# Loading chunk A ahead of chunk C, and bringing one row to all partitions by DMA instead of a matmul

## The chip, the cores and the metric

The kernel runs on one core of a Trainium2 chip. The metric is device time in microseconds (us).

Engines are written as the profile writes them: PE (TensorE, matmuls), PEld (its weight loads), DVE (VectorE), ACT (ScalarE), POOL (GpSimd), SP (SyncE, which issues the DMAs). "L717" is line 717 of the kernel whose profile is shown; after the change the same statement may have another number.

## The reference, cut to what matters

```python
# x: [8, 3008, 256] fp32
X = np.fft.fft(x, axis=1); X = np.fft.fft(X, axis=2)
y = X.real.reshape(8 * 3008, 256)
g = y @ w_gate                       # w_gate, w_val: [256, 1536]
out = (g / (1 + np.exp(-g)) * (y @ w_val)) @ w_out
```

The kernel never forms the spectrum in full. It folds x by symmetry (POOL), multiplies with cosine and sine tables (PE) to get two half spectra P and Q, and uses that rows k and M-k of the real part are P+Q and P-Q. So each column tile of P and Q gives two sets of outputs, "plus" and "minus". The second transform is folded into the weights (Wp, Wq, Wm).

## The kernel before

The main loop runs over 24 tiles t of up to 512 columns and 12 blocks f of the hidden size: 288 *units*. A unit computes gate g and value v for plus (`part_a`) and for minus (`part_b`, one unit later), and between them PE does four or eight output matmuls of the tile before (`owork.run(4)`). From tile 2 on, six of the twelve units (nine in the last tiles) are *split*: value is made of an even part e and an odd part o, so that DVE does three cheap combinations and POOL does the multiplies. Only these need `bc`, the row d=0 of Q copied to all partitions.

```python
psG: 3 PSUM banks (g)   psV: 3 PSUM banks (v, e, o)   psO: 2 banks
SPLIT = (0, 2, 3, 5, 7, 9)

def part_a(u):                                   # (cut)
    g = psG.tile(...);  mm(g, Wp, 0, Pt, True, False);  mm(g, Wq, 0, Qt, False, True)      # L717
    if split(u):
        e = psV.tile(...);  mm(e, Wp, 1, Pt, True, True)
        o = psV.tile(...);  mm(o, Wm, 1, Qt, True, True)     # "v<-Qt,Wm" in the profile
        sg = silu(g)                                                                       # ACT
        es = bc[t] * w0[:, f] + e                                                          # DVE L732
        vp = es - 0.5 * o;  vm = es + 0.5 * o (columns reversed)                           # DVE L734, L736
        hp = sg * vp                                                                       # POOL L737
        return
    v = psV.tile(...);  mm(v, Wp, 1, Pt, True, False);  mm(v, Wq, 1, Qt, False, True)
    hp = silu(g) * v                                                                       # ACT, DVE L745
# part_b(u), one unit later: adds Wm @ Qt to g (and, if not split, to v)                   # PE L754
#   split: hm = silu(g) * vm on POOL (L759);   else hm = silu(g) * v on DVE (L763)

for i, u in enumerate(units):                    # (cut)
    t, f = u
    if f == 0 and split((t, SPLIT[0])):
        ps = psG.tile([P, T], F32, name="g")
        nc.tensor.matmul(ps[:, :w], sel, pq_tiles(t)[1][:, :w], start=True, stop=True)     # L854, the row matmul
        bc[t] = bcp.tile([P, T], F32, name="bc")
        nc.scalar.copy(bc[t][:, :w], ps[:, :w])                                            # L857
    if i == 10:
        loads.extend((("A", 1), fn) for fn in load_a(1, nc.sync))
    run_loads(3)                                 # issue the next three queued loads
    part_a(u)
    if owork: owork.run(4)
    if prev is not None: part_b(prev) ...
    if owork ...: owork.run(4)
    for what, j in fold_at.get(i, ()): fold_step(what, j, i)      # POOL folds, a step at a time
```

Chunk A of a batch is 20 loads into `XA` (2 MB), chunk C is 20 smaller ones for each of two batches into `XC`. The fold of chunk A of batch 1 is spread over units 13 to 24; its first step issues all loads that are still queued in front of it. `XA` is first used for weights; its last reader is a group of small matmuls in unit 9.

Of the kernel before, what the change touches and what calls it, by code (L numbers as in the profile page):

```python
# [12 lines left out]
F32 = mybir.dt.float32  # L13
I32 = mybir.dt.int32
BF16 = mybir.dt.bfloat16
# [16 lines left out]
def kernel(  # L32
# [8 lines left out]
    nc = tc.nc  # L41
    B, M, D = x.shape
    Dff = moe_w_gate.shape[1]
    P = 128
# [5 lines left out]
    T = 512  # L50
# [6 lines left out]
    nT = len(wide)  # L57
# [9 lines left out]
    def width(t):  # L67
        return wide[t]

    def tile_of(c):  # L70
        return max(t for t in range(nT) if t0[t] <= c)
# [6 lines left out]
    psG = ctx.enter_context(tc.tile_pool(name="psG", bufs=3, space=bass.MemoryType.PSUM))  # L78
# [12 lines left out]
    sel = const.tile([P, P], BF16, name="sel")  # L91
# [21 lines left out]
    def rows_at(b, row, ap):  # L113
        return bass.AP(tensor=x.tensor, offset=(b * M + row) * D, ap=ap)

    def up_block(b, j, n):
        return rows_at(b, 2 * j - 1, [[2 * D, n], [R * D, 4], [1, 2 * D]])

    def down_set(b, a, j, L, n):

        return rows_at(b, R * (a + 1) - 2 * j, [[2 * L * D, n], [-2 * D, L], [1, 2 * D]])
# [3 lines left out]
    def load_a(b, q):  # L125
        X3 = XA.rearrange("p a q d -> p a (q d)")
        return ([lambda h=h: q.dma_start(out=X3[LA * h:LA * (h + 1), 0:4, :],
                                         in_=up_block(b, JA - LA * h, LA)) for h in range(NA)] +
                [lambda a=a: q.dma_start(out=X3[:, 4 + a, :], in_=down_set(b, a, JA, LA, NA)) for a in range(4)])
# [16 lines left out]
    def fold_steps(eng, X, CE, BB, q, r, given=None):  # L146
        tt = eng.tensor_tensor
        S, Dd = given or (SDf[r, 0], SDf[r, 1])
        E, O = EOf[r, 0], EOf[r, 1]

        def sd(a, op):
            tt(SDf[r, a], X[r, 0:4, q, :], X[r, 7:3:-1, 1 - q, :], op=op)  # L152

        def even():
            tt(E[:, :, 0:P], S[:, :, P:0:-1], S[:, :, P:D], op=Alu.add)
            eng.tensor_copy(E[:, :, P:P + 1], S[:, :, 0:1])

        def odd():
            tt(O[:, :, 0:P], Dd[:, :, P:0:-1], Dd[:, :, P:D], op=Alu.subtract)

        def ab():
            tt(Af[r], EOf[r, :, 0:2, :], EOf[r, :, 2:4, :], op=Alu.add)  # L162

        def ce():
            tt(CE[r, q, :, 0, :], Af[r, :, 0, :], Af[r, :, 1, :], op=Alu.add)
            tt(CE[r, q, :, 1, :], Af[r, :, 0, :], Af[r, :, 1, :], op=Alu.subtract)

        def bb():
            tt(BB[r, q, 0], E[:, 0:4:3, 0:P], E[:, 2:0:-1, 0:P], op=Alu.subtract)
            tt(BB[r, q, 1], O[:, 0:2, 0:P], O[:, 2:4, 0:P], op=Alu.subtract)  # L170
            tt(BB[r, q, 1, :, 0:1], S[:, 3::-3, 0:1], S[:, 1:3, 0:1], op=Alu.subtract)

        return [lambda: sd(0, Alu.add), lambda: sd(1, Alu.subtract), even, odd, ab, ce, bb]
# [3 lines left out]
    def coef_a(b):  # L177
        if b not in coefA:
            coefA[b] = (cp.tile([P, 2, 2, 2, P + 1], BF16, name="CEa"),
                        cp.tile([P, 2, 2, 2, P], BF16, name="BBa"))  # L180
        return coefA[b]

    def coef_c(b):
        p = b if b < 2 else 1 + b // 2
        if p not in coefC:
            coefC[p] = (cp.tile([P, 2, 2, 2, P + 1], BF16, name="CEc"),
                        cp.tile([P, 2, 2, 2, P], BF16, name="BBc"))
        return coefC[p]
# [40 lines left out]
    for hi in range(2):  # L229
        q.dma_start(out=XC3[64 * hi:64 * hi + NCR, 0:2, :],  # L230
                    in_=rows_at(0, 2 * (P + 1) - 1 + 2 * hi * R, [[2 * D, NCR], [R * D, 2], [1, 2 * D]]))
    for hi in range(2):
        for a in range(2):
            q.dma_start(out=XC3[64 * hi:64 * hi + NCR, 2 + a, :],
                        in_=down_set(0, 3 - 2 * hi - a, JC, LC, NC_))
    q.dma_start(out=XC0[NCR:64 + NCR + 1:64, 0:2, 1],
                in_=rows_at(0, 0, [[2 * R * D, 2], [R * D, 2], [1, D]]))
# [21 lines left out]
    for i in range(6):  # L259
        ps = psO.tile([P, T], F32, name="o")  # L260
# [99 lines left out]
    opposite(0)  # L360
    nc.vector.memset(EOf[:, 1, :, P:P + 1], 0.0)
    nc.vector.memset(Tab[:, :, :, :, NOO - 1:NOO], 0.0)
    nc.vector.memset(sel[0:1, :], 1.0)
    vts(m2, pcol, scalar1=0.0, scalar2=-2.0, op0=Alu.not_equal, op1=Alu.mult)
    vts(sgn, half, scalar1=1.0 / 32, scalar2=1.0, op0=Alu.mult, op1=Alu.add)
    vts(wC, pc, scalar1=float(LC - 1), scalar2=-0.5, op0=Alu.is_equal, op1=Alu.mult)
# [146 lines left out]
    def pq_tiles(t):  # L513
        if t not in ptile:
            w = width(t) + B if t == nT - 1 else T
            ptile[t] = (pqp if t < nT - 1 else const).tile([P, w], BF16, name="Pt")
            qtile[t] = (pqp if t < nT - 1 else const).tile([P, w], BF16, name="Qt")
        return ptile[t], qtile[t]
# [78 lines left out]
    def whole_part(b, part):  # L597
        transform(b, part, (0,))
        transform(b, part, (1,))
# [20 lines left out]
    bcp = ctx.enter_context(tc.tile_pool(name="bc", bufs=2))  # L620
# [77 lines left out]
    SPLIT = (0, 2, 3, 5, 7, 9)  # L698
    SPLIT_END = (0, 1, 2, 4, 5, 7, 8, 10, 11)
    t_end = tile_of((B - 1) * H) + 1  # L700

    bc = {}

    def split(u):

        return 2 <= u[0] < nT - 1 and u[1] in (SPLIT if u[0] < t_end else SPLIT_END)
# [41 lines left out]
    def part_b(u):  # L748
        t, f = u
        w = width(t)  # L750
        Pt, Qt = pq_tiles(t)
        g, v = state.pop(u)
        for gv, ps in ((0, g), (1, v))[:1 if split(u) else 2]:
            nc.tensor.matmul(ps[:, :w], Wm[:, gv, f * P:(f + 1) * P], Qt[:, :w], start=False, stop=True,  # L754
                             skip_group_check=True)
        if split(u):
            sg = sgv.tile([P, T], F32, name="sgv")
            nc.scalar.activation(sg[:, w - 1::-1], g[:, :w], AF.Silu)  # L758
            nc.gpsimd.tensor_tensor(hts[t][1][:, f, :w], sg[:, :w], v[:, :w], op=Alu.mult)  # L759
            return  # L760
        sg = sgp.tile([P, T], F32, name="sg")
        nc.scalar.activation(sg[:, :w], g[:, :w], AF.Silu)  # L762
        nc.vector.tensor_tensor(hts[t][1][:, f, w - 1::-1], sg[:, :w], v[:, :w], op=Alu.mult)  # L763
# [21 lines left out]
    act_at = {}  # L785

    def run_loads(n):
        for _, fn in loads[:n]:
            fn()
        del loads[:n]  # L790

    def fold_step(what, i, unit):
        kind, b = what
        q, j = divmod(i, 7)
        if i == 0:
            run_loads(max((k + 1 for k, (w_, _) in enumerate(loads) if w_ == what), default=0))
        if j == 0:
            if kind == "A":
                queue[what] = fold_steps(nc.gpsimd, XA, *coef_a(b), q, slice(0, P))
            else:  # L800
                queue[what] = fold_steps(nc.gpsimd, XC, *coef_c(b), q, slice(64 if b == 1 else 0, P))
        queue[what].pop(0)()
        if q == 1 and j == 1:
            act_at.setdefault(unit + 2, []).append(what)

    def load_next(what):
        kind, b = what
        if kind == "A":
            if b + 1 < B:
                loads.extend((("A", b + 1), fn) for fn in load_a(b + 1, nc.sync))  # L810
        else:
            b = b // 2 * 2 + 2
            if b < B:
                loads.extend((("C", b), fn) for fn in load_c(b, nc.sync) + load_c(b + 1, nc.sync))
# [30 lines left out]
    loads = []  # L845
# [2 lines left out]
    owork = None  # L848
    for i, u in enumerate(units):
        t, f = u  # L850
        if f == 0 and split((t, SPLIT[0])):
            ps = psG.tile([P, T], F32, name="g")
            w = width(t)
            nc.tensor.matmul(ps[:, :w], sel, pq_tiles(t)[1][:, :w], start=True, stop=True)  # L854
            bc.pop(t - 2, None)
            bc[t] = bcp.tile([P, T], F32, name="bc")
            nc.scalar.copy(bc[t][:, :w], ps[:, :w])  # L857
        for fn in before.pop(i, ()):
            fn()
        if i == 10:  # L860
            loads.extend((("A", 1), fn) for fn in load_a(1, nc.sync))
        run_loads(3)
        part_a(u)
        if owork:
            owork.run(4)
        if prev is not None:
            part_b(prev)
            if prev[1] == nF - 1:
                owork = OWork(prev[0], hts[prev[0]])
                owork.run(4)  # L870
        if owork and not (prev is not None and prev[1] == nF - 1):
            owork.run(4)
        for what, j in fold_at.get(i, ()):
            fold_step(what, j, i)
        for what in act_at.pop(i, ()):
            load_next(what)
        if i in job_at:
            whole_part(*job_at[i])
        prev = u
# [35 lines left out]
```

## Time and profile before

Median 712.93 us (3 runs, 712.68 to 713.99).

The page of the profile: span, busy time of PE and POOL, and the busy tenths of 40 slices of 17.8 us each:

```profile
span 712.3 us, 13268 instructions
PE 679.5 (95%) x4369; PEld 415.4 (58%) x4369; DVE 518.8 (73%) x925; ACT 433.6 (61%) x765; POOL 593.5 (83%) x577
...
PE   7879937999999999999999999999999999999997
...
POOL 7896199999999999999999889998899745657930
PEclk9989977999999999999999999999999999999999
```

After the start-up there is one large hole: PE falls to 3 tenths in the sixth slice, POOL to 1 in the fifth. The table by stretches (length, busy us and instructions of each engine, granted clock, DMA share, GB/s) puts it at 80 to 120 us, and shows PE otherwise busy almost always:

```profile
core 0: us, PE busy (x) PEld busy (x) DVE busy (x) ACT busy (x) POOL busy (x), PEclk, DMA share, GB/s
...
80.00:100.00 20.00, 15.12 (x98) 9.56 (x96) 9.96 (x15) 8.60 (x16) 13.22 (x13) 0.98 0.36 86
100.00:120.00 20.00, 9.16 (x37) 4.41 (x37) 5.55 (x9) 5.14 (x9) 19.76 (x19) 0.59 0.59 117
...
200.00:300.00 100.00, 99.72 (x647) 61.24 (x645) 77.37 (x135) 63.97 (x113) 97.70 (x91) 1.00 0.27 78
```

Who waited for whom from 60 to 130 us (total, times, longest). Read from the bottom: PE's g matmul waits for a bank that ACT must read, ACT waits for a buffer that POOL must read, and POOL had waited for a DMA. Releasers are inferred; the DMA that ended POOL's wait was the last load of chunk A (it landed at 86.0 us, and the fold that reads `XA` started at 86.5), not the output store that the first line names.

```profile
POOL SDf L152 <- DMA out_dram<-ev: 22.0, 1, 22.0
DVE vv L734 <- POOL hp L737: 16.6, 2, 15.1
...
ACT sgv L758 <- POOL hp L737: 15.2, 2, 14.8
PE g L717 <- ACT sgv L758: 13.5, 1, 13.5
```

The timeline of SP says why the data was late: the chunk A loads (L127, L129) stand behind chunk C loads that start only at 58.3 us, when POOL has read the rows they overwrite.

```profile
58.30 5.78 SPq L136 DMA_DIRECT2D XC<-in_x_dram  x15
64.27 3.57 SPq L138 DMA_DIRECT2D XC<-in_x_dram  x4
67.89 0.63 SPq L140 DMA_DIRECT2D XC<-in_x_dram  x1
69.18 7.64 SPq L127 DMA_DIRECT2D XA<-in_x_dram  x16
77.21 2.57 SPq L129 DMA_DIRECT2D XA<-in_x_dram  x4
```

Matmuls of 512 columns start 0.217 us apart when nothing stops PE.

### The profile page before, as it was taken

How to read it: one execution, taken by the hardware profiler on the slowest of the kernel's cores; microseconds unless marked ns; L12 is line 12 of the kernel's file. 1: busy time of each engine (PE TensorE's matmuls, PEld its weight loads, DVE VectorE, ACT ScalarE, POOL GpSimd, SP SyncE). 2: the span in 40 equal slices, each digit the busy share in tenths (PEclk: the TensorE clock that was granted, in tenths of full speed). 3: DMA queues.
4: the chain of work that ended last, by engine and by line, in shares of the span. 5: the costliest groups of instructions: out<-in, count | busy, mean ns of one | idle time of the engine just before them, and what ended most of it. 6: DMA issues, size and time to landing. Idle time of an engine off the chain costs nothing.

```text
span 712.3 us, 13268 instructions
## 1 busy us (share of the span) xinstructions
PE 679.5 (95%) x4369; PEld 415.4 (58%) x4369; DVE 518.8 (73%) x925; ACT 433.6 (61%) x765; POOL 593.5 (83%) x577
## 2 busy tenths in 40 slices
PE   7879937999999999999999999999999999999997
PEld 4435624556655656655665656656566556656676
DVE  8776615768777787777877777777777777878862
ACT  7565614556655666656666656656566556656663
POOL 7896199999999999999999889998899745657930
PEclk9989977999999999999999999999999999999999
DMA  9652716133241521324315211114211111101112
GB/s 216 118 86 64 153 20 141 45 93 93 74 118 31 131 64 52 105 76 104 92 44 128 66 39 37 45 41 127 71 40 37 46 31 45 45 30 46 37 55 68
DMA packets 45567, 52.55 MB, mean 74 GB/s; under 512 B 6290, under 2 KB 33466, under 8 KB 45498
## 3 DMA queue, kind: packets, MB, share of 16 engines
q1 hardware_dynamic: 42314, 49.35, 25.6%
q0 software_dynamic: 3184, 2.36, 2.4%
q8 instruction: 34, 0.56, 0.3%
q14 instruction: 35, 0.29, 0.1%
HBM read 29.39 MB, written 24.65 MB: 76 GB/s over the span
## 4 chain that ended last, share of the span: by engine, by line
PE 76%; DMA 7%; POOL 7%; DVE 3%; issue 3%; SPq 2%; ACT 0%; POOLq 0%; ACTq 0%; DVEq 0%
PE o L677 31%; PE v L717 15%; PE g L717 14%; PE g L754 8%; DMA XC<-in_x_dram 3%; POOL SDf L152 3%; PE v L754 3%; PE g L566 3%; PE v L566 3%; DVE vv L736 2%; DMA XA<-in_x_dram 2%; DMA XC_107<-in_x_dram 1%; DVE vv L734 1%; SPq L138 1%; POOL Af L162 1%
## 5 line engine op out<-in xcount | busy, mean ns | idle before, releaser
L737 POOL TENSOR_TENSOR hp<-sgv,vv 128x512 bf16<-128x512 f32 (+1 forms) x132 | 167.6, 1271 | 49.3 <-DVE vv L734 37.6
L759 POOL TENSOR_TENSOR hm<-sgv,vv 128x512 bf16<-128x512 f32 (+1 forms) x132 | 167.2, 1271 | 8.5 <-ACT sgv L758 8.1
L677 PE MATMUL o<-Wo,hp 128*128 128x256 bf16 (+2 forms) x1140 | 170.7, 274 | 0.0
L677 PE MATMUL o<-Wo,hm 128*128 128x256 bf16 (+2 forms) x1140 | 169.6, 273 | 0.0
L677 PEld LDWEIGHTS <-hp 128*128 128x128 bf16 (+2 forms) x1140 | 112.5, 99 | 70.8 <-issue 11.4
L677 PEld LDWEIGHTS <-hm 128*128 128x128 bf16 (+2 forms) x1140 | 111.8, 98 | 64.9 <-issue 5.5
L732 DVE SCALAR_TENSOR_TENSOR es<-bc,w_85,v 128x512 f32<-128x512 f32 (+1 forms) x132 | 98.1, 743 | 51.5 <-PE v L717 51.1
L745 DVE TENSOR_TENSOR hp<-sg,v 128x512 bf16<-128x512 f32 (+2 forms) x156 | 103.6, 664 | 34.9 <-ACT sg L744 34.1
L717 PE MATMUL g<-Pt,Wp 128*128 128x512 bf16 (+2 forms) x288 | 108.7, 377 | 13.6 <-ACT sgv L758 13.5
L744 ACT ACTIVATE sg<-g 128x512 f32<-128x512 f32 (+2 forms) x156 | 90.9, 583 | 45.5 <-PE g L717 40.5
L758 ACT ACTIVATE sgv<-g 128x512 f32<-128x512 f32 (+1 forms) x132 | 78.9, 598 | 64.9 <-PE g L754 41.9
L762 ACT ACTIVATE sg<-g 128x512 f32<-128x512 f32 (+2 forms) x156 | 91.1, 584 | 43.5 <-PE g L754 43.2
L763 DVE TENSOR_TENSOR hm<-sg,v 128x512 bf16<-128x512 f32 (+2 forms) x156 | 103.1, 661 | 19.1 <-ACT sg L762 8.6
L734 DVE SCALAR_TENSOR_TENSOR vv<-v,es 128x512 f32<-128x512 f32 (+1 forms) x132 | 91.1, 690 | 34.8 <-POOL hp L737 16.9
L754 PE MATMUL g<-Qt,Wm 128*128 128x512 bf16 (+2 forms) x288 | 108.6, 377 | 5.2 <-ACT sg L744 5.2
L717 PE MATMUL v<-Pt,Wp 128*128 128x512 bf16 (+2 forms) x288 | 108.7, 377 | 0.6 <-DVE vv L736 0.6
L717 PE MATMUL g<-Qt,Wq 128*128 128x512 bf16 (+2 forms) x288 | 108.7, 377 | 0.5 <-DVE Qt L579 0.5
L729 ACT ACTIVATE sgv<-g 128x512 f32<-128x512 f32 (+1 forms) x132 | 78.7, 596 | 45.3 <-PE g L717 35.6
L736 DVE SCALAR_TENSOR_TENSOR vv<-v,es 128x512 f32<-128x512 f32 (+1 forms) x132 | 89.7, 679 | 8.1 <-POOL hm L759 5.2
L152 POOL TENSOR_TENSOR SDf<-XA 128x1024 f32<-128x1024 f32 x28 | 66.0, 2360 | 23.2 <-DMA out_dram<-ev 22.0
L717 PEld LDWEIGHTS <-Wp 128*128 128x128 bf16 x576 | 56.5, 98 | 42.0 <-issue 5.6
L683 ACT COPY ev<-o 128x512 f32<-128x512 f32 x90 | 52.7, 585 | 31.4 <-PE o L677 29.7
(173 smaller groups left out, 740.4 us busy)
## 6 DMA issues: line engine op xcount, KB each, us to landing
out_dram<-ev SPq DMA_DIRECT2D x96, 128.0 KB
XA<-in_x_dram SPq DMA_DIRECT2D x32, 256.0 KB
XA<-in_x_dram SPq DMA_DIRECT2D x112, 64.0 KB
XC<-in_x_dram SPq DMA_DIRECT2D x105, 32.0 KB
XC<-in_x_dram SPq DMA_DIRECT2D x28, 120.0 KB
out_dram<-ev SPq DMA_DIRECT2D x12, 120.0 KB
out_dram<-ev SPq DMA_DIRECT2D x10, 112.0 KB
XA<-in_x_dram SPq DMA_DIRECT2D x1, 1024.0 KB
```

The source lines that it names most:

```text
L677: nc.tensor.matmul(ps[:n, j, :], hts[minus][:, f, c:c + n], Wo[:, f, :], start=(f == 0), stop=(f == nF - 1))
L717: nc.tensor.matmul(ps[:, :w], Wt[:, gv, fs], src[:, :w], start=start, stop=stop, skip_group_check=True)
L732: stt(es[:, :w], bc[t][:, :w], w0[:, f:f + 1], e[:, :w], op0=Alu.mult, op1=Alu.add)
L734: stt(vp[:, :w], o[:, :w], -0.5, es[:, :w], op0=Alu.mult, op1=Alu.add)
L736: stt(vm[:, w - 1::-1], o[:, :w], 0.5, es[:, :w], op0=Alu.mult, op1=Alu.add)
L737: nc.gpsimd.tensor_tensor(hts[t][0][:, f, :w], sg[:, :w], vp[:, :w], op=Alu.mult)
L744: nc.scalar.activation(sg[:, :w], g[:, :w], AF.Silu)
L745: nc.vector.tensor_tensor(hts[t][0][:, f, :w], sg[:, :w], v[:, :w], op=Alu.mult)
L754: nc.tensor.matmul(ps[:, :w], Wm[:, gv, f * P:(f + 1) * P], Qt[:, :w], start=False, stop=True, skip_group_check=True)
L759: nc.gpsimd.tensor_tensor(hts[t][1][:, f, :w], sg[:, :w], v[:, :w], op=Alu.mult)
L762: nc.scalar.activation(sg[:, :w], g[:, :w], AF.Silu)
L763: nc.vector.tensor_tensor(hts[t][1][:, f, w - 1::-1], sg[:, :w], v[:, :w], op=Alu.mult)
```

## The change

Intent: have chunk A of batch 1 in place before POOL needs it, and take the 21 row matmuls from PE and the 21 copies from ACT.

```diff
-    nc.vector.memset(sel[0:1, :], 1.0)
...
+    rowd = tc.dram_tile([nT, T], BF16, name="rowd")
...
         if q == 1 and j == 1:                    # queue the next loads after the fold has read its input
-            act_at.setdefault(unit + 2, []).append(what)
+            act_at.setdefault(max(unit + 2, 11), []).append(what)
...
-        if f == 0 and split((t, SPLIT[0])):
-            ps = psG.tile([P, T], F32, name="g")
-            w = width(t)
-            nc.tensor.matmul(ps[:, :w], sel, pq_tiles(t)[1][:, :w], start=True, stop=True)
-            bc.pop(t - 2, None)
-            bc[t] = bcp.tile([P, T], F32, name="bc")
-            nc.scalar.copy(bc[t][:, :w], ps[:, :w])
+        if f == 10 and t + 1 < nT and split((t + 1, SPLIT[0])):
+            bc.pop(t - 1, None)
+            bc[t + 1] = bcp.tile([P, T], BF16, name="bc")
+            w = width(t + 1)
+            nc.sync.dma_start(out=rowd[t + 1:t + 2, :w], in_=pq_tiles(t + 1)[1][0:1, :w])
+            nc.sync.dma_start(out=bc[t + 1][:, :w], in_=rowd[t + 1:t + 2, :w].to_broadcast([P, w]))
...
         if i == 10:
-            loads.extend((("A", 1), fn) for fn in load_a(1, nc.sync))
+            loads[0:0] = ((("A", 1), fn) for fn in load_a(1, nc.sync))
```

Before, everything queued in front of chunk A was flushed with it at unit 13. Now chunk A is in front, and the chunk C loads follow at three per unit from unit 14.

## The prediction

> **What bounds the kernel now.** TensorE. The page gives PE 95% busy, VectorE 73%, ScalarE 61%, GpSimd 83%. In the table by stretches PE is busy 99.3 to 100% of every stretch from 120 to 600 us. The exception is one hole: in 80 to 120 us PE is busy only 24.3 of 40 us. The waits in that stretch name the chain: PE's g matmul waits 13.5 us in one piece (95.2 to 108.7 us) for ScalarE's sgv, which waits 14.8 us for GpSimd's hp multiply. The GpSimd timeline shows why: after the first chunk-C fold ends at 64.5 us it idles 22.0 us, because chunk A of batch 1 lands only at about 86.4 us; its fold (86.5 to 109.5 us) then stands in front of the split units' multiplies. The SyncE timeline shows the cause: those 20 loads are issued at 69.2 to 79.8 us, behind 20 chunk-C loads that cannot start before 58.3 us, when the fold of the C rows that they overwrite has ended.
>
> **What the change does.**
> 1. Chunk A's loads go first. Their target is last read at 49.8 us (value-row matmuls), so they can issue from about 50 us. Before, first issue to last landing took 16.8 us; the same from 50 us gives landing at about 67 us, and the fold starts there instead of at 86.5: about 19 us earlier. The first split multiply then comes at about 87 us, where PE's first split unit (84.3 us) needs it.
>    The hole costs 13.5 us, 2.2 us in smaller waits, and about 2.8 us of half-rate matmuls after it (0.43 us apart instead of 0.22 until 116.5 us; granted clock 0.50). Together about 18.5 us, nearly all on the critical path. I give 2.5 us back: the delayed chunk-C loads now finish at about 93 us by my count, so GpSimd waits briefly there.
> 2. The 21 row matmuls go, 0.217 us apart each: 4.5 us of PE time, on the critical path because PE is full. The 21 ScalarE copies (585 ns each, 12 us) also go, but ScalarE has slack: worth nothing. VectorE's es (743 ns) reads bf16 instead of fp32: I expect no change.
> 3. Two serial DMAs per tile come in. In the trace an unloaded store lands 1.3 to 1.9 us after issue, a chunk load under traffic 3 to 6 us. The Trainium skill, "DMA: Bandwidth & Descriptors", section "Anatomy of one DMA", puts a fixed cost of about 2 us mostly on the write receipt (for the GpSimd path); the SyncE stores here agree in size. So the row needs about 3.6 us unloaded, and its lead is two units, about 4.3 us at 2.17 us each. Tight: where load bursts or a blocked in-order SyncE queue meet it, es comes late. PSUM buffers absorb about one unit. I add 2 us in all.
>
> **Sum.** 712.9 - 18.5 + 2.5 - 4.5 + 2 = 694.4 us.
>
> Predicted 694.4 us, range 687 to 705. Chances: faster by over 2% 0.74, within 2% 0.23, slower by over 2% 0.03.
>
> **What would show it.** Right: GpSimd's 22 us idle before the chunk-A fold shrinks below 4 us; the 13.5 us PE wait disappears; PE is above 95% in 80 to 120 us; no row matmul; es waits for its own matmul, not for DMA.
> Wrong: a new PE hole around 90 to 105 us (late chunk C), or VectorE's es waiting for the row's DMA by over 2 us in many tiles, followed by PE waits for es or vv.
>
> **What would make it wrong.** The row's DMA latency: 3 us of stall in each of 21 tiles would eat everything. Or GpSimd, 98 to 100% busy in 160 to 300 us, becoming the limit once PE is quicker.

## More of the kernel before

One more place matters later: unit 0 of a tile in the steady state. This is PE's timeline there (start, duration; tile 19), with the row matmul L854:

```profile
571.25 0.60 PE L677 MATMUL o<-Wo,hm 128*128 128x256 bf16 x4
571.68 0.38 PE L854 MATMUL g<-Qt,sel 128*128 128x512 bf16 x1
571.90 0.38 PE L717 MATMUL g<-Pt,Wp 128*128 128x512 bf16 x1
572.11 0.38 PE L717 MATMUL g<-Qt,Wq 128*128 128x512 bf16 x1
572.33 0.38 PE L717 MATMUL v<-Pt,Wp 128*128 128x512 bf16 x1
572.60 0.38 PE L717 MATMUL v<-Qt,Wm 128*128 128x512 bf16 x1
```

and DVE's at the same moment (hm of the unit two before, which reads a v bank):

```profile
571.86 0.69 DVE L763 TENSOR_TENSOR hm<-sg,v 128x512 bf16<-128x512 f32 x1 [0.39 <-PE o L677]
```

## The result, and the profile after

Median 705.02 us (4 runs, 703.53 to 705.80); the kernel before, in the same rounds, 713.23 us (4 runs). The ratio is 0.9882, 95% interval 0.9862 to 0.9901. The prediction was 694.4 us with a range of 687 to 705 and 74% for "faster by over 2%". The measured gain of 1.2% is less than half of the 2.6% that was forecast. The same lines of the page as before:

```profile
span 703.5 us, 13284 instructions
PE 678.7 (96%) x4348; PEld 413.6 (59%) x4348; DVE 518.9 (74%) x924; ACT 423.4 (60%) x744; POOL 593.6 (84%) x577
...
PE   7879979999999999999999999999999999999997
...
POOL 7996989899999899999998989998899645657930
PEclk9979998999999999999999999999999999999999
```

PE no longer has a 3, and POOL no longer has a 1. The table by stretches:

```profile
80.00:100.00 20.00, 19.31 (x123) 11.99 (x121) 12.87 (x20) 10.36 (x19) 16.59 (x17) 1.00 0.43 110
100.00:120.00 20.00, 16.63 (x94) 8.73 (x93) 11.93 (x27) 9.47 (x17) 19.49 (x20) 0.83 0.49 124
...
200.00:300.00 100.00, 98.72 (x632) 59.34 (x631) 74.91 (x130) 60.61 (x106) 96.06 (x90) 1.00 0.30 82
```

The large hole is gone. Two things are not as forecast: 100 to 120 us still has 3.4 us without PE at a clock of 0.83, and in 200 to 300 us PE is *less* busy than before although it has less to do. The POOL timeline shows the first: chunk A's fold now starts at 69.5 us, 17 us earlier, but POOL still has to wait twice (the bracket gives the idle time before the instruction). What it waits for is told by what the instruction reads: the first reads `XA`, so chunk A, and the second `XC`, so chunk C. The DMAs that the brackets name are inferred, and here they are not those.

```profile
63.04 0.20 POOL L171 TENSOR_TENSOR BBc<-SDf 64x2 bf16<-64x2 f32 x1
69.47 4.67 POOL L152 TENSOR_TENSOR SDf<-XA 128x1024 f32<-128x1024 f32 x2 [6.23 <-DMA XC<-in_x_dram]
...
89.78 1.28 POOL L737 TENSOR_TENSOR hp<-sgv,vv 128x512 bf16<-128x512 f32 x1
...
96.77 2.35 POOL L152 TENSOR_TENSOR SDf<-XC 128x1024 f32<-128x1024 f32 x1 [3.02 <-DMA XA<-in_x_dram]
```

Waits after 130 us show that DVE's es now waits for the row's DMA in eleven tiles:

```profile
DVE es L732 <- DMA bc<-rowd: 10.9, 11, 2.0
```

And this is unit 0 of tile 19 again on PE's timeline, without the row matmul:

```profile
562.10 0.60 PE L676 MATMUL o<-Wo,hm 128*128 128x256 bf16 x4
562.54 0.38 PE L717 MATMUL g<-Pt,Wp 128*128 128x512 bf16 x1
562.76 0.38 PE L717 MATMUL g<-Qt,Wq 128*128 128x512 bf16 x1
562.97 0.38 PE L717 MATMUL v<-Pt,Wp 128*128 128x512 bf16 x1
563.46 0.38 PE L717 MATMUL v<-Qt,Wm 128*128 128x512 bf16 x1
```

DVE's timeline at the same moment:

```profile
562.72 0.69 DVE L763 TENSOR_TENSOR hm<-sg,v 128x512 bf16<-128x512 f32 x1 [0.40 <-ACT sg L762]
```

Look at the last matmul, o. Before it starts 0.27 us after the one ahead of it (572.33 to 572.60), now 0.49 us (562.97 to 563.46). In both cases it starts 0.05 us after DVE's hm has ended (571.86 + 0.69 = 572.55; 562.72 + 0.69 = 563.41). The bank of o is the one that hm reads: units 10 and 11 of the tile before are not split and take one v bank each, unit 0 takes two, and psV has three. So o of unit 0 cannot start before hm of unit 10 has ended, whether or not PE does a row matmul while it waits. That matmul used 0.217 us of a wait of about 0.27 us. The wait is nearly invisible in the busy shares: the span of e ends at 563.35 (562.97 + 0.38), so only 0.11 us of the 0.27 us shows as idle.

To see where the time went I took from both traces the start of the first g matmul of each of the 288 units, and compared the length of each unit. This is worked out from the PE records, not a view of the profile. "Length" is the distance to the next unit's start; the table gives the length after minus the length before, in us, for unit 11 of the tile before (whose end the row matmul occupied) and units 0 to 8.

```
tile   u11    u0     u1     u2     u3     u4     u5     u6     u7     u8
  2  -0.22   0.22   0.40   0.19   0.26 -13.65  -3.55   0.17   3.19   0.93
  4  -0.22   0.22   0.81   0      0.43   0      0      0      0      0
  7  -0.22   0.22   0.43   0      0.10   0      0      0      0      0
 12  -0.22   0.21   0      0      0      0      0      0      0      0
 18  -0.22   0.21   0      0      0      0      0      0      0      0
 20  -0.22   0.22   0      0      0      0      0      0      0      0
 21  -0.22   0.22   0.45   0      0      0      0      0      0      0
```

In 20 of the 21 tiles the 0.22 us of the removed matmul is won at the end of unit 11 and lost again in unit 0, to within 0.01 us. Adding up over the kernel, where the normal length of a unit is taken from later tiles (1.95 us where the unit before is split, 2.17 us where it is not, since part_b of that unit falls into it):

| | us |
|---|---|
| start-up, up to unit 12 (in other runs it varies by over 1 us either way) | -0.6 |
| old hole removed: units 28 to 31 took 27.6 us before, normal 8.2 | +19.3 |
| new hole in units 30 to 32: 12.5 us, normal 6.1 | -6.4 |
| row matmuls removed, 21 of 0.217 us | +4.6 |
| the same, given back in unit 0 | -4.3 |
| units 1 to 3 longer, in tiles 2, 4, 7, 14, 21 and 22 | -3.8 |
| rest | -0.1 |
| sum, to the start of the last unit | +8.7 |

The table says where; what caused each line had to be tried.

### The profile page after: what moved, and what is told of

Read it like the earlier page. It is cut to its first block, busy times and chain, and to the rows that moved or that the text cites. A ratio compares the mean times of both kernels' runs of the same rounds, so it can differ in the third digit from the quotient of the medians.

```text
span 703.5 us, 13284 instructions
## 1 busy us (share of the span) xinstructions
PE 678.7 (96%) x4348; PEld 413.6 (59%) x4348; DVE 518.9 (74%) x924; ACT 423.4 (60%) x744; POOL 593.6 (84%) x577
## 4 chain that ended last, share of the span: by engine, by line
PE 74%; DVE 8%; DMA 7%; issue 4%; POOL 3%; ACT 2%; SPq 1%; DVEq 0%; POOLq 0%; ACTq 0%
PE o L676 29%; PE v L717 15%; PE g L717 13%; PE g L754 7%; DMA XC<-in_x_dram 3%; PE v L754 3%; PE g L565 3%; DVE vv L736 3%; PE v L565 3%; DVE hm L763 2%; ACT sg L762 1%; DMA bc<-rowd 1%; POOL SDf L152 1%; DMA rowd<-Qt 1%; DMA XC_107<-in_x_dram 1%
## 5 line engine op out<-in xcount | busy, mean ns | idle before, releaser
L676 PEld LDWEIGHTS <-hm 128*128 128x128 bf16 (+2 forms) x1140 | 112.3, 99 | 71.4 <-issue 12.5
L732 DVE SCALAR_TENSOR_TENSOR es<-bc,w_85,v 128x512 f32<-128x512 bf16 (+1 forms) x132 | 98.1, 743 | 56.8 <-PE v L717 38.1
L763 DVE TENSOR_TENSOR hm<-sg,v 128x512 bf16<-128x512 f32 (+2 forms) x156 | 103.2, 661 | 19.0 <-ACT sg L762 16.8
```

What stands on the lines that cost most here:

```text
L676: nc.tensor.matmul(ps[:n, j, :], hts[minus][:, f, c:c + n], Wo[:, f, :], start=(f == 0), stop=(f == nF - 1))
L732: stt(es[:, :w], bc[t][:, :w], w0[:, f:f + 1], e[:, :w], op0=Alu.mult, op1=Alu.add)
L763: nc.vector.tensor_tensor(hts[t][1][:, f, w - 1::-1], sg[:, :w], v[:, :w], op=Alu.mult)
```

## The experiments

My theory after this reading: (a) the row matmuls were free, since they ran in a wait for a v bank; (b) the row DMAs cost some 3 us because rows come late; (c) the load order gives all of the gain, and what is left of the hole is POOL being late. The rival to (a) and (b): the removal did give 4.5 us, and the load order gave less than it seems.

All kernels gave correct outputs. Times are medians, with the ratio to the kernel before in the same rounds.

| run | us | ratio | 95% interval |
|---|---|---|---|
| the change | 705.02 | 0.9882 | 0.9862 to 0.9901 |
| e1 order only | 701.35 | 0.9837 | 0.9780 to 0.9894 |
| e2 rows only | 716.33 | 1.0068 | 1.0019 to 1.0117 |
| e3 filler in unit 0 | 706.17 | 0.9916 | 0.9872 to 0.9960 |
| e4 filler in unit 6 | 710.13 | 0.9970 | 0.9924 to 1.0017 |
| e5 rows early | 703.01 | 0.9845 | 0.9800 to 0.9891 |
| e6 chunk C flushed | 711.90 | 0.9983 | 0.9944 to 1.0022 |
| e7 output matmuls between e and o | 701.62 | 0.9841 | 0.9804 to 0.9877 |
| e8 the same with the row matmul | 696.28 | 0.9762 | 0.9720 to 0.9803 |
| e9 = e5 and e7 | 694.98 | 0.9737 | 0.9699 to 0.9774 |
| e10 = e9 and late split | 691.98 | 0.9703 | 0.9661 to 0.9745 |
| e11 = e10 with the row matmul | 692.61 | 0.9688 | 0.9654 to 0.9722 |
| e12 = e10, tile 3's row by matmul | 689.04 | 0.9662 | 0.9638 to 0.9687 |

e1 to e4 shared a chip, so did e5 to e8, and e9 to e11.

### e1 and e2: the two halves of the change alone

e1 is the kernel before with the `max(unit + 2, 11)` and `loads[0:0]` lines of the diff only; e2 is the kernel before with all the rest of the diff.

> Only the new load order; the row matmul and its copy stay. Theory (the row matmul sits in time in which PE waits for a PSUM bank of v anyway, so its removal gave nothing, and the row DMAs cost about 3 us through late rows): about 701 us, so 4 us faster than the whole change. Rival (the removal gave its 4.5 us, the load order gave less than it seems): about 709 us.

> Only the row by DMA; the old load order stays. Theory: 714 to 716 us, the same or slower than before (713.2), with the o matmul of unit 0 waiting about 0.27 us in nearly every tile instead of 0.05. Rival: about 709 us, the 4.5 us of the removed matmuls.

Measured: 701.35 us and 716.33 us. The load order alone is 11 us faster than before on that chip; the row DMAs alone are 4 us slower than before (0.7%, and the interval lies above 1). e2 is just beyond its expected range. In its trace DVE's es waits 18.6 us for the row's DMA, 17 times. The halves add up to roughly the whole (-11.0 and +4.0, against -8.2 for the change). The rival's 709 us for each is missed by over 7 us both times. In e1 POOL hardly waits before chunk C's fold:

```profile
96.61 2.35 POOL L152 TENSOR_TENSOR SDf<-XC 128x1024 f32<-128x1024 f32 x1 [0.47 <-DMA XC<-in_x_dram]
```

### e3 and e4: put 21 useless matmuls back, in two places

```diff
         g = psG.tile([P, T], F32, name="g")
+        if f == 0 and 2 <= t < nT - 1:          # e4: f == 6
+            nc.tensor.matmul(g[:, :w], sel, Qt[:, :w], start=True, stop=True, skip_group_check=True)
         mm(g, Wp, 0, Pt, True, False)           # overwrites it
```

> The whole change, with 21 useless 128x512 matmuls put back where the row matmul was, at the start of unit 0, into the g bank that the next matmul overwrites. Theory (they fill a wait): within 0.7 us of the change (705.0). Rival (PE is full there): 4.5 us slower, 709.5 us.

> The same 21 useless matmuls at the start of unit 6, where the trace of the change shows no wait of PE. Both theories: 4.5 us slower than the change, 709.5 us. With the unit 0 filler at no cost this shows that it is the place that makes the matmul free. If this one is free as well, PE is not the limit anywhere and the theory falls.

Measured: 706.17 us and 710.13 us, 4.0 us apart on the same chip. e4 came out as expected; e3 missed its range by 0.5 us. The medians alone leave doubt for e3 (its ratio is 0.3% above that of the change, on another chip), and tile 2 disturbs both traces: es waits there for its row up to 4.9 us in e3 and 6.1 us in e4. So here are unit lengths again, taken from the first value matmul of each unit, each minus the same of the change:

```
            e3, filler in unit 0              e4, filler in unit 6
tile     u11    u0     u1    u6           u11    u0     u1    u6
  6     0.22  -0.21    0     0             0      0      0    0.21
 12     0.22  -0.22    0     0             0      0      0    0.22
 18     0.22  -0.22    0     0             0      0      0    0.22
 20     0.22  -0.22    0     0             0      0      0    0.22
```

From tile 6 to tile 22 e3 falls behind the change by 0.10 us in all, e4 by 3.6 us (16 tiles of 0.217 us are 3.5). The same matmul is free in unit 0 and costs its full pace in unit 6. This settles (a) for these tiles: PE is the limit, but not in unit 0, where it waits for a PSUM bank.

### e5: the rows earlier

```diff
-        if f == 10 and t + 1 < nT and split((t + 1, SPLIT[0])):
+        if f == (10 if t == 2 else 7) and t + 1 < nT and split((t + 1, SPLIT[0])):
```

> The whole change, with each row's two DMAs three units earlier (unit 7 instead of 10; for tile 3, whose data is finished only in unit 9, still unit 10). Theory (late rows cost 3 to 4 us: about 1.0 at tile 2, 1.3 at tile 4, 1.6 in the rest): VectorE's es waits for the row's DMA under 3 us in all instead of 10.9, and the kernel takes 701 to 703 us beside 705. Rival (the waits of es are all absorbed by buffers): no change.

Measured: 703.01 us, and no wait of es for the row's DMA is left in the table of waits. From unit 60 to 264 it takes 468.4 us against 470.6 for the change; the kernel before takes 469.3 there. So with rows in time the DMA way is a little better than the matmul, by 0.9 us in 17 tiles, and with rows at unit 10 it is worse by 1.3. This confirms (b): against the change, units 1 to 3 become 3.9 us shorter in all. It also rules out that late rows were why unit 0 gave the 0.22 us back, since with the rows in time unit 11 is still 0.22 us shorter, and unit 0 0.22 us longer, than in the kernel before. The trace of the change gives the sizes of the DMAs: from issue to the last semaphore update the row's store takes 1.42 us and the broadcast load 2.91 us in the median of 21 (1.08 to 2.58, and 2.85 to 3.64), one after the other, against a lead of two units, 4.1 us.

### e6: chunk C right behind chunk A, a miss

```diff
-        run_loads(3)
+        run_loads(len(loads) if i == 14 else 3)
```

> The whole change, but all chunk C loads are queued at unit 14, right behind chunk A, instead of three per unit. Theory (the rest of the hole, 4.3 us in units 30 to 33, comes from GpSimd waiting 3.0 us for chunk C before its fold): GpSimd's wait of 3.0 us goes to under 0.5, the hole shrinks by 2 to 3 us, 702 to 703 us. Rival (the rest of the hole comes from chunk A's fold ending too late): under 1 us.

Measured: 711.90 us, worse than the change by 7 us, which neither theory had. POOL's wait before chunk C is gone, but the row of tile 2 now stands behind 40 loads and nine output stores in the same in-order queue. SP's timeline:

```profile
91.84 0.64 SPq L140 DMA_DIRECT2D XC<-in_x_dram  x1
92.59 3.65 SPq L688 DMA_DIRECT2D out_dram<-ev  x9
96.34 0.25 SPq L856 DMA_DIRECT2D rowd<-Qt  x1
97.89 0.35 SPq L857 DMA_DIRECT2D bc<-rowd  x1
```

and the waits from 60 to 130 us:

```profile
DVE es L732 <- DMA bc<-rowd: 15.4, 1, 15.4
...
PE v L717 <- DVE es L732: 14.0, 1, 14.0
POOL SDf L152 <- DMA XC<-in_x_dram: 10.1, 1, 10.1
```

In the change the row's store was issued at 82.5 us, here at 96.3. So a hole as large as the old one opens, for a new reason. The question that e6 was to answer stays open in it; e10 answers a part of it. The last line also shows chunk A landing later (POOL waits 10.1 us for it, 6.2 in the change): from first issue to last landing it took 22.1 us here, 18.2 in the change, 20.3 in e1, before anything else was queued differently. I have not explained this spread.

### e7 and e8: fill the wait at unit 0 (and at unit 3) with other work

The change's trace (and the one before) has the same kind of wait at unit 3, 0.28 us on average in 16 tiles: there o starts 0.05 us after DVE's vm of unit 2, which reads the o of that unit. Here four output matmuls, which PE would do right after, go between e and o.

```diff
+            if between:
+                between()                        # owork.run(4)
             o = psV.tile([P, T], F32, name="v")
...
-        part_a(u)
-        if owork:
+        mid = bool(owork) and f in (0, 3) and split(u)
+        part_a(u, (lambda: owork.run(4)) if mid else None)
+        if owork and not mid:
             owork.run(4)
```

> The whole change, with four output matmuls moved between the e and o matmuls of units 0 and 3, so that PE has work while the bank of o is still being read. Theory: the waits of 0.27 us at unit 0 and 0.28 us at unit 3 go in some 20 tiles each: 8 to 10 us faster, 695 to 697 us. Rival (VectorE or GpSimd limits as soon as PE does not wait): 1 to 3 us.

> The same move of output matmuls, but with the row matmul and its copy kept (new load order only). Theory: the unit 3 waits go (5 us), at unit 0 only 0.05 us per tile is left to win, as the row matmul already fills that wait: 5 to 6 us faster than the load order alone, and PE now pays 4.5 us for the row matmuls that the other kernel of this pair does not have.

Measured: e8 696.28 us, 5.1 below e1, as expected. e7 701.62 us, only 3.4 below the change, a miss of 5 us. The trace of e7 says why: the waits at units 0 and 3 are gone, but es now waits 17.8 us for rows (10.9 in the change), up to 4.5 us in tile 2, and PE waits 7.9 us for es. A quicker PE makes the lead of two units shorter.

### e9, e10, e11: all together, with and without the row matmul

e9 joins e5 and e7. e10 also keeps units 0, 2, 3 and 5 of tile 2 unsplit, so that POOL has no multiplies behind the fold of chunk A (the condition for the rows is adapted, so that tile 2 still gets its row):

```diff
     def split(u):
+        if u[0] == 2 and u[1] < 7:
+            return False
```

e11 is e10 with the row matmul and copy in place of the DMAs (that is, e8 with the late split).

> The whole change with rows three units earlier and four output matmuls between e and o. Theory (the removal of the row matmul is worth its 4.5 us once the wait at unit 0 is filled otherwise and the row is in time): VectorE's waits for the row's DMA vanish (17.8 us with the output matmuls moved alone), 692 to 694 us, about 3 to 4 us faster than the same with the row matmul kept (696.3). Rival (GpSimd or VectorE limits by then): 696 us or more.

> As e9, and in tile 2 the units 0, 2, 3 and 5 are not split, so GpSimd has no multiplies there while it folds chunk A. Theory (the rest of the hole, about 4 us in units 30 to 33, is GpSimd's backlog): the hole goes, 3 to 4 us faster than e9, 688 to 691 us. Rival (the rest of the hole is something else, as the slow clock after it): under 1 us.

> As e10 but with the row by matmul and copy at unit 0. Beside e10 on the same chip it prices the row matmuls where nothing hides them: 4 to 4.5 us slower than e10 by the theory (21 times 0.217 us, less what the wait at unit 0 still hides); the same as e10 if the matmuls stay hidden or the DMAs cost as much.

Measured: 694.98, 691.98 and 692.61 us. Each of the first two is about 1 us above its expected range. e9 was also to be 3 to 4 us faster than e8; the medians, on two chips, give 1.3 us, and the intervals of the ratios overlap. In the two traces unit 11 is 0.20 to 0.22 us shorter in e9 in each tile from 2 to 21, with nothing given back in unit 0.

The hole: units 24 to 33 take 31.5 us in the change, 32.3 in e9 and 32.9 in e8, and 25.2 in both e10 and e11, of which only 0.5 us is above normal. So (c) is right: what was left of the hole was POOL's multiplies waiting behind the folds, and it goes when they are taken away, although POOL still waits for chunk C in e10 (4.9 us):

```profile
98.78 4.67 POOL L152 TENSOR_TENSOR SDf<-XC 128x1024 f32<-128x1024 f32 x2 [4.90 <-DMA XC<-in_x_dram]
```

The price of the row matmul, e10 against e11, was forecast as 4 to 4.5 us and came out as 0.6 us in the medians (the ratios of means put e11 ahead by 0.15%, so the order isn't clear of noise). The unit lengths show two parts. In each tile from 4 to 21 e10's unit 11 is 0.217 us shorter than e11's, and nothing is given back in unit 0. But in unit 1 of tile 3 e10 loses 4.0 us at once: that row's data is finished only in unit 9 of tile 2, so its DMAs could not go early. DVE's timeline in e10 there:

```profile
117.68 0.71 DVE L736 SCALAR_TENSOR_TENSOR es<-bc,w,v 128x480 f32<-128x480 bf16 x1 [3.50 <-DMA bc<-rowd]
```

### e12: tile 3's row by matmul, the others by DMA

```diff
+        if f == 0 and t == 3:
+            (the row matmul and the copy of the kernel before, into a bf16 bc)
-        if f == (10 if t == 2 else 7) and 2 <= t + 1 < nT - 1:
+        if f == 7 and 2 <= t + 1 < nT - 1 and t != 2:
```

> As e10, but the row of tile 3 alone comes by matmul and copy (its data is ready only in unit 9 of the tile before, and by DMA it arrived 3.5 us late and cost PE 4 us in unit 1 of tile 3). Theory: VectorE's wait for the row's DMA goes from 3.5 us to none, PE's unit 1 of tile 3 takes 1.9 us instead of 5.9, and the kernel takes about 688 us, ratio to before about 0.965, beside 0.970 for e10: then removing the other 19 or 20 row matmuls pays its 0.217 us per tile. Rival (the 4 us come back later): 691 to 692 us.

Measured: 689.04 us (6 runs, 688.02 to 690.41), ratio 0.9662, about 1 us above the expectation. Unit 1 of tile 3 takes 1.89 us instead of 5.88, and no wait of es for the row's DMA is left. Of the 4.0 us, 1.8 come back in units 4 and 5 of tile 5, which take that much longer than in e10; this isn't explained. Against e11, which keeps all row matmuls, e12's trace is 1.8 us shorter from unit 24 on, and in whole times the intervals of the two ratios overlap: the 0.217 us per tile is shown in the traces, and its worth for the whole kernel is not. This is the fastest version: 24 us faster than before in its rounds, three times the gain of the change.

## Why the prediction was wrong

Step by step, as the prediction put them:

1. *"The hole costs ... Together about 18.5 us, nearly all on the critical path."* Right: 19.3 us by unit lengths. PE's 13.5 us wait is gone, POOL's 22.0 us of idle time has shrunk to 6.2 us (the prediction named under 4 us as a sign of being right), and e1 shows that the load order alone does it.
2. *"I give 2.5 us back"* for the late chunk C. Right in kind, too small: the new hole, which the prediction had named as a sign of being wrong, is 6.4 us. Chunk C was counted to finish at about 93 us, and POOL could start its fold only at 96.8 us, after a wait of 3.0 us. Chunk A also landed 2 us later than counted (first issue to last landing 18.2 us, not 16.8, and it began 0.75 us later), so its fold ended at 92.5 us. The split multiplies stand behind both folds; the next one after the wait started at 99.1 us. In the change the chain that ended last runs through the landing of chunk C, so the wait for it was on the path. But it was not needed for the hole: e1 has the same hole with a wait of 0.5 us (the line shown under e1), because its chunk A landed 2.4 us later and kept POOL busy until 96.1 us. e10 removes the hole by removing the multiplies. How the 6.4 us divide between the two chunks no run shows.
3. *"4.5 us of PE time, on the critical path because PE is full."* This is the step that failed: the removed matmuls were not on the critical path. The gain was 0.2 us. PE was "full" only in the sense of the busy share. In unit 0 it was waiting for a v bank, and the row matmul ran inside that wait: 0.22 us was won in unit 11 and lost in unit 0, in 20 of 21 tiles. e3 and e4 show it (the same matmul is free in unit 0, and costs 0.22 us per tile in unit 6). The work only becomes worth removing when the wait is filled otherwise: e10 against e11 has 0.217 us per tile with nothing given back.
   The Trainium skill bears on this. "Perfetto Trace Analysis", section "Identifying the Most-Contended Engine", says that matmul busy share is not a good measure of how close a kernel is to roofline, because pipelined matmuls look smaller in the trace. Here they looked larger, not smaller (spans of 0.38 us, starts 0.217 us apart), and so the busy share hid waits; no run here measures the distance to roofline. Its section "Optimization Strategy" says that a gap that repeats on the engine that should be saturated can mean that there is not enough SBUF or PSUM for the next tile. This agrees with that: after the change PE, 98.7% busy from 200 to 300 us, had waits of 0.27 us at unit 0 and 0.28 us (on average) at unit 3 in nearly every tile, both for one of three v banks. Filling the one at unit 3 was worth 5 us in e8 (at unit 0 the row matmul left only 0.05 us), and filling both about 8 us in e9 (695.0 beside 703.0 for e5, on another chip).
4. *"I add 2 us in all"* for late rows. Right in kind, too small: up to 3.8 us, by the units 1 to 3 of six tiles. "About 3.6 us unloaded" was 4.3 us (1.42 and 2.91 us), while the lead was about 4.1.
5. *"ScalarE ... worth nothing"*, and es no faster from bf16: right. es took 743 ns before and after.

The sum: 4.3 us from step 3, 3.9 from step 2, 1.8 from step 4, 0.6 from start-up, less 0.8 that the old hole was worth more than predicted, make 9.8 us of the 10.6 by which the prediction missed. So step 3 is the largest part, and step 2 is nearly as large.

That (b) holds rests on e5 and its trace, and (c) on e8 to e11. That the removed row matmul was inside the wait rests on e3, e4 and e5. What is not settled: how the new hole divides between the late chunk A and the late chunk C, and why chunk A takes between 18 and 22 us to land when nothing else is in its way.

## What to carry to other kernels

Before counting removed work as gained, look at the start-to-start distances on the limiting engine around it: if the engine waits for a buffer a few instructions later, the removed work may have been running inside that wait, and then its removal only makes the wait longer. Put filler there and elsewhere to see which it is. Where a small DMA that others wait for is issued by the same engine as the bulk loads, as here, its lead has to be counted from when that engine reaches it (13.9 us later in e6 than in the change), and the lead shrinks when the compute gets faster (e7).

## What the Trainium skill lacked or had wrong

- "Perfetto Trace Analysis", "Optimization Strategy": it tells to look for gaps between slices. Here a wait of 0.27 us left a gap of 0.11 us between the shown spans, since matmuls 0.217 us apart have spans of 0.38 us. The page doesn't say to take start-to-start distances for PE, which showed the wait in full.
- "DMA: Bandwidth & Descriptors", "Anatomy of one DMA": its fixed cost of about 2.0 us is fitted for the GpSimd path, and the page fits none for SyncE. Here one row of 1 KB took 1.42 us from SyncE's issue to the last semaphore update (store to DRAM, median of 21). The broadcast of one such row to 128 partitions took 2.91 us; the page gives no time for a broadcast load.
- No page that I read warns that a latency-critical small DMA waits behind bulk loads in SyncE's issue order by as much as in e6: issued 13.9 us later (96.3 us instead of 82.5), es waiting 15.4 us.
